# Lightning attention and a low-rank mixer: the state's product with 128 columns of weights, and mixing from two copies of V

## The chip, the cores and the metric
The kernel runs on one core of a Trainium2 chip. The metric is the time of one execution on the device, in microseconds (us).

## The reference
Four batches of 768 positions and 8 heads of 64 go through a decayed linear attention, in blocks of 64 positions. The result, read as x with 512 channels, is mixed along the sequence by a matrix of rank 32, and a two-layer network with a ReLU follows. Everything is fp32.

```python
for b in range(nb):                       # blocks of 64 positions, every head
    intra = einsum('bhic,bhjc->bhij', qb, kb) * Dmask       # decayed, causal
    intra = einsum('bhij,bhjd->bhid', intra, vb)
    inter = einsum('bhid,bhde->bhie', qb * lam_pow, kv_state)
    out[:, :, sl] = intra + inter
    kv_state = lam_block * kv_state + einsum('bhsd,bhse->bhde', kb_dec, vb)

x  = out.transpose(0, 2, 1, 3).reshape(4, 768, 512)
xt = x.transpose(0, 2, 1)
h  = xt @ U @ V                           # U: 768 x 32, V: 32 x 768
u  = x + h.transpose(0, 2, 1)
return u + maximum(u @ w_ch1, 0) @ w_ch2  # 512 -> 2048 -> 512
```

U, V and the two weights arrive as 8-byte floats, and the kernel makes fp32 values of them.

## The kernel before, in words
The kernel has three stretches. In the first (up to about 117 us) attention runs in `NS` = 24 steps s, each for 128 positions of one batch (c = s mod 6 counts the steps of a batch), and the mixing of the batch before runs between its pieces. In the second the first layer of the network runs, with matmuls of 128x128 weights against 512 columns, while the second layer's weights are prepared. In the third the second layer runs. Values that need more than the fast matmul type (`F32R`) holds are split in a high and a low part, and the products of the parts are summed.

In the first stretch the order on every engine is written out by hand: the loop that fills `pieces` lists the functions of a step, and each function issues its instructions at once. An engine works through its instructions in that order. For TensorE a middle step is: transposes of q and k for step s+1 (`prep`, L358), transposes of an earlier x (`turn`, L608), the mixing product of a step six or seven back (`mix`, L559), the masked scores times v (`intra`, L447), the new state (`state`, L425), the queries times the old state (`inter`, L458), and the scores of step s+1 (`scores`, L406). At the end of a batch `low` (L474) multiplies U by the batch's x.

The array of TensorE is used in parts. A form such as 64*128 in the profile says that weights of 64 rows and 128 columns are held. Heads lie in pairs: heads 2a and 2a+1 lie in the two halves of the 128 partitions (`half[x]`). `scores` uses 64*128: each half of the rows has one head's 64 channels, and the columns are 128 positions. `inter` uses 64*64: for each pair a and head x it issues one matmul for each half t of the 128 positions. It is left out in the first step of a batch (c = 0), where the state is zero. `px` takes both `intra` and `inter`, and ScalarE copies it to `x_nat` (L464), which frees it for the next step.

The mixing works in this way. `low_rows` splits the batch's low-rank part (32 x 512) into high and low parts and puts them in `p_hl`, a tile of 128 partitions x 512. For batches 0 to 2 the 512 channels are two halves of 256 that go to the two halves of the partitions. In each half the 32 rows of the high part stand twice, one below the other, in columns 0 to 255, and the 32 rows of the low part stand twice in columns 256 to 511. This is done by three small functions that `next_of_low` calls one after the other: `spread` (L527, four ScalarE casts), `low_part` (L531, two GpSimd subtractions) and `spread_low` (L538, two ScalarE casts). `v_hl` holds V in the four groups of 32 partitions: high, low, high, low. `mix` multiplies one 64-row half of V's 128 columns by each part of `p_hl`: four matmuls a step. `mixed` (L571, VectorE) adds the product to x. The last batch is mixed later, with one matmul of 128 rows a step (L566).

V is prepared by `v_steps` in the first steps: the loads, the conversion, then `five` (L699), the four ScalarE copies of its high part (L706), and the two calls of `low` (L710), of which one runs on VectorE and one on GpSimd. The table beside it puts both calls of `low` at the end of step 5. The first mixing product comes in step 7.

All loads and stores of this stretch go out through the queue of SyncE (SP), which takes its instructions in order: q, k and v of a later step (L279), the words of the weights (L140), and the stores of x (`u_d`, L577).

Of the kernel before, what the change touches and what calls it, by code (L numbers as in the profile page):

```python
# [8 lines left out]
FP32 = mybir.dt.float32  # L9
F32R = mybir.dt.float32r  # L10
# [4 lines left out]
P = 128  # L15
# [3 lines left out]
def kernel(  # L19
# [28 lines left out]
    nc = tc.nc  # L48

    B, H, S, D = q.shape  # L50
    HP = H // 2
    NT = S // P
    C = H * D
# [34 lines left out]
    def set_ends(t):  # L88
        nc.vector.memset(t[:, 0:1], 1151.0)
        nc.vector.memset(t[:, 1:2], 255.0 * (1 << 23))  # L90
        ends.append(t)
# [195 lines left out]

    assert G == 4
    vp = w1_pool.tile([P, 3, C], F32R, tag="w1", name="vp").rearrange("p n c -> p (n c)")
    v_hl, p_hl = vp[:, 0:S], vp[:, S : S + C]  # L290


    ident = keep.tile([P, P], FP32, name="ident")
    small = consts.tile([P, 16], FP32, name="small")
    zeros = small[:, 0:1]

    mask = consts.tile([P, 2, HP, P], FP32, name="mask")
# [154 lines left out]
    def inter(s):  # L452

        px = st[s]["px"][:, :, 0 : HP * D].rearrange("p x (a e) -> p x a e", a=HP)
        for a in range(HP if s % NT else 0):
            for x in range(2):
                for t in range(2):
                    nc.tensor.matmul(  # L458
                        out=px[half[t], x, a, :], lhsT=st[s]["qs"][half[x], a, half[t]],
                        rhs=kv[s][half[x], a, :], start=False, stop=(a == HP - 1),  # L460
                    )
        pool, tag = (att, "x10") if s % 10 == 5 else (x_pool, "x")
        xs[s] = pool.tile([P, C], FP32, tag=tag, name="x_nat")
        nc.scalar.copy(xs[s].rearrange("p (a x e) -> p x a e", a=HP, x=2), px)  # L464
        del st[s]
# [21 lines left out]
    def low_rows(b):  # L487

        pp, t = pps.pop(b), tmp("p_h")[0:R]
        own = [(slice(g * R, (g + 1) * R), slice(g * P, (g + 1) * P)) for g in range(G)]  # L490
        if b == B - 1:
            h, h2, l, l2 = (p_hl[g * R : (g + 1) * R] for g in range(G))
            for rows, cols in own:
                nc.vector.tensor_scalar(
                    t[:, cols].bitcast(U32), pp[rows].bitcast(U32), HI, None, ALU.bitwise_and
                )

            def low_part():
                for rows, cols in own:
                    nc.vector.tensor_tensor(  # L500
                        out=l[:, cols], in0=pp[rows], in1=t[:, cols], op=ALU.subtract
                    )

            def spread():
                nc.scalar.copy(h, t)
                nc.scalar.copy(h2, t)

            def spread_low():
                nc.scalar.copy(l2, l.bitcast(FP32))

            pps[b] = [spread, low_part, spread_low]
            return

        rows_f, pp = pp, others.pop(b)
        for g in range(2, G):
            nc.vector.tensor_copy(
                out=rows_f[:, g * P : (g + 1) * P], in_=pp[g * R : (g + 1) * R]
            )
        nc.vector.tensor_scalar(t.bitcast(U32), rows_f.bitcast(U32), HI, None, ALU.bitwise_and)
        wide = [slice(x * 2 * P, (x + 1) * 2 * P) for x in range(2)]  # L520

        def place(g, low):
            return p_hl[g * R : (g + 1) * R, wide[low]]

        def spread():
            for g in range(G):
                nc.scalar.copy(place(g, 0), t[:, wide[g // 2]])  # L527

        def low_part():
            for x in range(2):  # L530
                nc.gpsimd.tensor_tensor(  # L531
                    out=place(2 * x, 1), in0=rows_f[:, wide[x]], in1=t[:, wide[x]],
                    op=ALU.subtract,
                )

        def spread_low():
            for x in range(2):
                nc.scalar.copy(place(2 * x + 1, 1), place(2 * x, 1).bitcast(FP32))  # L538

        pps[b] = [spread, low_part, spread_low]  # L540

    def next_of_low(b):
        pps[b].pop(0)()
# [7 lines left out]

    def mix(s):
        b, c = divmod(s, NT)
        weights = v_hl[:, c * P : (c + 1) * P]
        if b < B - 1:
            pm = both_halves(s)[:, :, 2 * P :]
            for low in range(2):
                for x in range(2):
                    nc.tensor.matmul(  # L559
                        out=pm[:, x], lhsT=weights[half[x]],  # L560
                        rhs=p_hl[half[x], low * 2 * P : (low + 1) * 2 * P],
                        start=(low == 0), stop=(low == 1),
                    )
            return
        pu = bank([P, C], "pu", "b2")
        nc.tensor.matmul(out=pu, lhsT=weights, rhs=p_hl, start=True, stop=True)  # L566
        nc.vector.tensor_tensor(out=xs[s], in0=pu, in1=xs[s], op=ALU.add)

    def mixed(s):
# [68 lines left out]
    for s in range(NS):  # L638
        b, c = divmod(s, NT)
        done = s - NT - 1  # L640
        more = s + 1 < NS
        turns = done > 0 and (done - 1) // TG < FG
        mixes = 0 <= done < NS - NT - 1
        rows = c == 0 and b > 0
        step = [("prep", s + 1)] * more
        step += [("turn", done - 1)] * turns + [("mix", done)] * mixes
        step += [("mix", done + 1)] * (not more)
        step += [("next_of_low", b - 1)] * rows + [("next_of_low", b - 1)] * rows
        step += [("scale", s + 1)] * more
        step += [("fade", s)] * (c > 0)  # L650
        step += [("late", s - 1)] * (1 < s < NT - 1 or s > NT)
        step += [("turned", done - 2)] * (done > 1 and c == 1)
        step += [("split", done - 1)] * turns
        step += [("mixed", done)] * mixes + [("mixed", done + 1)] * (not more)
        step += [("next_of_low", b - 1)] * rows
        both = [("intra", s), ("state", s)]
        step += (both if s > NT else both[::-1]) + [("next_v", s), ("inter", s)]
        step += [("late", s)] * (s < 2 or s in (NT - 1, NT))
        step += [("turned", done - 1)] * (done > 0 and c > 0)
        step += [("scores", s + 1)] * more  # L660
        step += [("low", b)] * (more and c == NT - 1)
        step += [("aside", s)] * (0 < s < NT - 2 or s > NT)
        step += [("masked", s + 1)] * more
        step += [("low_rows", b)] * (more and c == NT - 1)
        step += [("aside", s)] * (s in (0, NT - 2, NT - 1, NT))
        step += [("store", done)] * (done >= 0 and done // TG < FG)
        pieces += step
# [14 lines left out]
    def v_steps():  # L682

        st = {}

        def dst():
            if "v" not in st:
                st["v"] = wconv.tile([P, C], FP32, tag="wf", name="vf")[0 : 2 * R, 0:SH]
            return st["v"]

        def parts(gs):
            for half in range(2):
                rows, cols = slice(half * R, (half + 1) * R), slice(half * SH, (half + 1) * SH)
                for g in gs:
                    yield v_hl[g * R : (g + 1) * R, cols], rows

        def five():
            st["t"] = t = wconv.tile([P, C], FP32, tag="wt", name="vt")[0 : 2 * R, 0:SH]
            nc.vector.tensor_scalar(  # L699
                t.bitcast(U32), st["v"].bitcast(U32), HI, None, ALU.bitwise_and  # L700
            )
            on_scalar(high)

        def high():
            for out, rows in parts((0, 2)):
                nc.scalar.copy(out, st["t"][rows])  # L706

        def low(g, engine):
            for out, rows in parts((g,)):
                engine.tensor_tensor(  # L710
                    out=out, in0=st["v"][rows], in1=st["t"][rows], op=ALU.subtract
                )

        halves = [moe_V[:, half * SH : (half + 1) * SH] for half in range(2)]
        return weight_steps(dst, halves, SH, 2 * R, in_parts=True) + [
            five, lambda: low(1, nc.vector), lambda: low(3, nc.gpsimd),
        ]
# [26 lines left out]

    ordered = ctx.enter_context(ExitStack())
    ordered.enter_context(tc.manual_schedule())
    lam_row = consts.tile([1, H + P], FP32, name="lam_row")
    blank = x_pool.tile([P, C], FP32, tag="x", name="blank")[:, 0:P]
    nc.vector.memset(blank, 0.0)
    nc.vector.memset(lam_row[:, H:], 1.0)  # L750
    set_ends(vp[:, S + C : S + C + 2].bitcast(FP32))
    nc.scalar.dma_start(out=lam_row[:, 0:H], in_=lam.unsqueeze(0))
    load_next("q", nc.sync)
    load_next("k", nc.scalar)
# [299 lines left out]
```

## Time and profile before

| | us |
|---|---|
| median of 3 runs | 667.36 (666.33 to 668.0) |
| the profiled execution | 669.62 |
| its span, first to last instruction | 667.8 |
| `intra` L447, 768 matmul records, mean | 0.225 |
| `inter` L458, 640 records, mean | 0.225 |
| `scores` L406, 384 records, mean | 0.291 |
| `mix` L559, 72 records, mean | 0.320 |
| ScalarE's casts to `p_hl`, L527 x12 and L538 x6, mean | 0.403 |

Matmuls are pipelined and their ends are modelled, so a mean is longer than the distance from one matmul to the next. How long a group holds TensorE is read from the starts of the groups in the order of time. A row of the order in time has the start, the length of the group, the engine, the line, the operation, the tiles written and read, the shapes and the number of records. PEld is the loading of weights, which goes on beside the matmuls.

### The profile page before, as it was taken

The numbers are of one execution on the slowest core, as the hardware profiler recorded it, in microseconds if no ns is written. First come the engines' busy times: TensorE is split into PE (matmuls) and PEld (weight loads), VectorE is DVE, ScalarE is ACT, GpSimd is POOL, SyncE is SP. The second block draws the span as 40 slices with busy tenths as digits, with TensorE's granted clock in tenths as the row PEclk, the third lists the DMA queues.
The fourth block names the chain that finished last, engine by engine and source line by source line (L and its number), as shares of the span: only waits on it lengthen the run. The fifth ranks groups of instructions, "written<-read, shape, count | busy, mean of one in ns | idle before, by whom it ended". The sixth has DMA issues, their size and how long they took to land.

```text
span 667.8 us, 13404 instructions
## 1 busy us (share of the span) xinstructions
PE 656.2 (98%) x5242; PEld 538.7 (81%) x5242; DVE 491.0 (74%) x862; ACT 280.4 (42%) x530; POOL 115.0 (17%) x98
## 2 busy tenths in 40 slices
PE   8899999999999999999999999999999999999997
PEld 7788988788888888888888887888888888888886
DVE  5578988878999777777797255786677776865864
ACT  4677885554555444444453121332322322322320
POOL 4465876330000000000000000030030300300300
PEclk9999999999999999999999999999999999999999
DMA  8999984355776655555578899764263453543531
GB/s 197 224 224 233 259 217 139 127 190 162 268 249 238 216 199 202 201 201 200 201 263 292 311 326 395 253 212 126 89 211 104 125 190 94 168 147 96 159 93 63
DMA packets 131776, 131.29 MB, mean 197 GB/s; under 512 B 81346, under 2 KB 89794, under 8 KB 131714
## 3 DMA queue, kind: packets, MB, share of 16 engines
q1 hardware_dynamic: 130512, 130.05, 62.2%
q8 instruction: 41, 0.67, 0.4%
q10 hardware_dynamic: 1202, 0.39, 0.2%
q14 instruction: 21, 0.17, 0.1%
HBM read 80.09 MB, written 50.33 MB: 195 GB/s over the span
## 4 chain that ended last, share of the span: by engine, by line
PE 95%; DMA 1%; DVE 1%; SPq 1%; issue 1%; ACT 0%; DVEq 0%; ACTq 0%
PE pz L817 27%; PE pz L950 13%; PE pz L952 13%; PE pd L827 13%; PE pd L954 13%; PE px L447 3%; PE pss L406 3%; PE px L458 2%; PE pqk L358 2%; DMA qraw<-in_q_dram 1%; PE pkv L425 1%; SPq L279 1%; PE pp L474 1%; PE pm L559 1%; PE put L590 1%
## 5 line engine op out<-in xcount | busy, mean ns | idle before, releaser
L817 PE MATMUL pz<-u_hl,w 128*128 128x512 f32 x768 | 190.0, 397 | 0.0
L817 PEld LDWEIGHTS pz<-u_hl,w 128*128 128x128 f32 x768 | 144.0, 188 | 35.2 <-ACT r L823 0.3
L952 PE MATMUL pz<-w_hl,m 128*128 128x512 f32 x384 | 151.1, 396 | 0.0
L950 PE MATMUL pz<-w_hl,m 128*128 128x512 f32 x384 | 150.9, 396 | 0.0
L954 PE MATMUL pd<-w_d,m 128*128 128x512 f32 x384 | 149.5, 396 | 0.0
L933 ACT ACTIVATE m<-mt 128x512 fp32r<-128x512 f32 x96 | 60.6, 632 | 196.6 <-PE pd L954 127.5
L979 POOL TENSOR_TENSOR o<-o,u 128x512 f32<-128x512 f32 x20 | 29.9, 1531 | 447.4 <-DMA rm<-r_d 291.4
L934 DVE SCALAR_TENSOR_TENSOR m<-rm,m 128x512 fp32r<-128x512 f32 x96 | 71.4, 745 | 47.3 <-ACT m L933 47.2
L832 DVE SCALAR_TENSOR_TENSOR r<-pd,r 128x512 f32<-128x512 f32 x96 | 61.8, 685 | 53.5 <-ACT r L823 43.5
L827 PE MATMUL pd<-u_d,w 128*128 128x512 f32 x384 | 98.6, 397 | 0.0
L823 ACT ACTIVATE r<-pz 128x512 f32<-128x512 f32 x96 | 52.1, 596 | 93.0 <-PE pz L817 92.3
L952 PEld LDWEIGHTS pz<-w_hl,m 128*128 128x128 f32 x384 | 72.3, 188 | 17.8 <-DVE m L934 0.2
L954 PEld LDWEIGHTS pd<-w_d,m 128*128 128x128 f32 x384 | 72.3, 188 | 17.7 <-DVE m L935 0.2
L950 PEld LDWEIGHTS pz<-w_hl,m 128*128 128x128 f32 x384 | 72.3, 188 | 17.6
L827 PEld LDWEIGHTS pd<-u_d,w 128*128 128x128 f32 x384 | 72.1, 188 | 17.3
L932 DVE TENSOR_SCALAR mt<-rm 128x512 uint32<-128x512 uint32 x96 | 46.1, 481 | 33.5 <-DMA rm<-r_d 33.2
L935 DVE SCALAR_TENSOR_TENSOR m<-m 128x512 fp32r<-128x512 f32 x96 | 69.1, 721 | 0.9
L415 DVE TENSOR_TENSOR sm<-pss,mask 128x512 f32<-128x512 f32 x48 | 30.9, 684 | 10.0 <-PE pss L406 9.7
L212 ACT CAST w<-wt 128x512 fp32r<-128x512 f32 x32 | 19.8, 620 | 30.6 <-DVE wt L209 23.4
L406 PE MATMUL pss<-qt,kt 64*128 64x128 f32 x384 | 29.1, 291 | 0.8 <-issue 0.7
L447 PE MATMUL px<-vraw,sm 128*64 128x64 f32 x768 | 27.8, 225 | 1.2 <-ACT x_nat L464 0.6
L447 PEld LDWEIGHTS px<-vraw,sm 128*64 128x64 f32 x768 | 24.9, 138 | 3.9 <-ACT x_nat L464 0.9
(96 smaller groups left out, 668.7 us busy)
## 6 DMA issues: line engine op xcount, KB each, us to landing
r_d<-r SPq DMA_DIRECT2D x96, 256.0 KB, 2.4
rm<-r_d SPq DMA_DIRECT2D x96, 256.0 KB, 2.7
words<-in_moe_w_ch_dram SPq DMA_DIRECT2D x30, 512.0 KB, 4.3
w_d<-w SPq DMA_DIRECT2D x16, 768.0 KB, 3.3
w_hl<-w_d SPq DMA_DIRECT2D x16, 512.0 KB, 6.4
vraw<-in_v_dram SPq DMA_DIRECT2D x24, 256.0 KB, 5.0
u_d<-x_nat SPq DMA_DIRECT2D x24, 256.0 KB, 4.1
u<-u_d SPq DMA_DIRECT2D x24, 256.0 KB, 4.1
```

Source lines behind the costliest of these rows:

```text
L406: nc.tensor.matmul(out=pss[:, x, a, :], lhsT=kt[half[x], a, :], rhs=qt[half[x], a, :], start=True, stop=True,)
L447: nc.tensor.matmul(out=px[half[t], x, a, :], lhsT=sm[:, x, a, half[t]], rhs=vr[:, 2 * a + x, :], start=(a == 0), stop=(alone and a == HP - 1),
L817: nc.tensor.matmul(out=acc[g][0], lhsT=w[:, n, ct, :], rhs=uhl[g][:, n, ct, :], start=(ct == 0 and n == 0), stop=(ct == CT - 1 and n == 1),)
L823: nc.scalar.mul(rs[g], acc[g][0], 4096.0 + 1.0)
L827: nc.tensor.matmul(out=acc[g][1], lhsT=w[:, 2, ct, :], rhs=ud[g][:, ct, :], start=(ct == 0), stop=(ct == CT - 1),)
L832: nc.vector.scalar_tensor_tensor(rs[g], acc[g][1], 4096.0, rs[g], ALU.mult, ALU.add)
L933: nc.scalar.activation(out=m[:, 0], in_=t, func=AF.Relu)
L934: nc.vector.scalar_tensor_tensor(m[:, 1], r, 0.0, hi, ALU.max, ALU.subtract)
L935: nc.vector.scalar_tensor_tensor(m[:, 2], hi, E, low, ALU.mult, ALU.subtract)
L950: nc.tensor.matmul(out=pz, lhsT=m[:, 0, cols], rhs=hl[:, 0], start=first, stop=False)
L952: nc.tensor.matmul(out=pz, lhsT=m[:, 1, cols], rhs=hl[:, 1], start=False, stop=end)
L954: nc.tensor.matmul(out=pd, lhsT=m[:, 2, cols], rhs=dd, start=first, stop=end)
```

## The change
Three things are changed in the first stretch.

`inter` issues one matmul for each pair a and head x with all 128 positions as columns of weights. It has 8 matmuls a step where it had 16.

`mix` keeps its four matmuls but multiplies another pairing. `v_hl` becomes 128 x 2 x 768: in copy 0 the groups are V's high, low, high, low as before, in copy 1 they are low, high, low, high. `p_hl` becomes 128 x 256, with high and low one below the other in each half of the partitions. One matmul with copy 0 gives high x high and low x low, and one with copy 1 gives low x high and high x low. Copy 1 is made by four DMAs from copy 0 within SBUF (`swap`), issued on SP at the head of step 6. `spread` has two casts in place of four, and `spread_low` is gone.

The places of some small things move: `p_hl` gets a tile of its own, the row for `lam` goes to an unused part of the tile `blank`, and the two constants of `set_ends` go to the tile `small`. The last batch puts its low-rank part where copy 1 of V was.

```diff
-    v_hl, p_hl = vp[:, 0:S], vp[:, S : S + C]
+    v_hl = vp.rearrange("p (n c) -> p n c", n=2)
+    p_hl = consts.tile([P, 2 * P], F32R, name="p_hl")
...
-    small = consts.tile([P, 16], FP32, name="small")
+    small = consts.tile([P, 18], FP32, name="small")
...
             for x in range(2):
-                for t in range(2):
-                    nc.tensor.matmul(
-                        out=px[half[t], x, a, :], lhsT=st[s]["qs"][half[x], a, half[t]],
-                        rhs=kv[s][half[x], a, :], start=False, stop=(a == HP - 1),
-                    )
+                nc.tensor.matmul(
+                    out=px[:, x, a, :], lhsT=st[s]["qs"][half[x], a, :],
+                    rhs=kv[s][half[x], a, :], start=False, stop=(a == HP - 1),
+                )
...
-            h, h2, l, l2 = (p_hl[g * R : (g + 1) * R] for g in range(G))
+            h, h2, l, l2 = (v_hl[g * R : (g + 1) * R, 1, 0:C] for g in range(G))
...
-        def place(g, low):
-            return p_hl[g * R : (g + 1) * R, wide[low]]
+        def place(g):
+            return p_hl[g * R : (g + 1) * R]
 
         def spread():
-            for g in range(G):
-                nc.scalar.copy(place(g, 0), t[:, wide[g // 2]])
+            for x in range(2):
+                nc.scalar.copy(place(2 * x), t[:, wide[x]])
 
         def low_part():
             for x in range(2):
                 nc.gpsimd.tensor_tensor(
-                    out=place(2 * x, 1), in0=rows_f[:, wide[x]], in1=t[:, wide[x]],
+                    out=place(2 * x + 1), in0=rows_f[:, wide[x]], in1=t[:, wide[x]],
                     op=ALU.subtract,
                 )
 
-        def spread_low():
-            for x in range(2):
-                nc.scalar.copy(place(2 * x + 1, 1), place(2 * x, 1).bitcast(FP32))
-
-        pps[b] = [spread, low_part, spread_low]
+        pps[b] = [spread, low_part]
...
-        weights = v_hl[:, c * P : (c + 1) * P]
+        weights = v_hl[:, :, c * P : (c + 1) * P]
         if b < B - 1:
             pm = both_halves(s)[:, :, 2 * P :]
-            for low in range(2):
+            for n in range(2):
                 for x in range(2):
                     nc.tensor.matmul(
-                        out=pm[:, x], lhsT=weights[half[x]],
-                        rhs=p_hl[half[x], low * 2 * P : (low + 1) * 2 * P],
-                        start=(low == 0), stop=(low == 1),
+                        out=pm[:, x], lhsT=weights[half[x], n], rhs=p_hl[half[x]],
+                        start=(n == 0), stop=(n == 1),
                     )
             return
         pu = bank([P, C], "pu", "b2")
-        nc.tensor.matmul(out=pu, lhsT=weights, rhs=p_hl, start=True, stop=True)
+        nc.tensor.matmul(out=pu, lhsT=weights[:, 0], rhs=v_hl[:, 1, 0:C], start=True, stop=True)
...
-        step = [("prep", s + 1)] * more
+        step = [("swap", s)] * (s == NT) + [("prep", s + 1)] * more
...
-        step += [("next_of_low", b - 1)] * rows
...
+        def swap():
+            whole = v_hl.bitcast(FP32)
+            for g in range(G):
+                nc.sync.dma_start(
+                    out=whole[g * R : (g + 1) * R, 1],
+                    in_=whole[(g ^ 1) * R : ((g ^ 1) + 1) * R, 0],
+                )
...
-    lam_row = consts.tile([1, H + P], FP32, name="lam_row")
-    blank = x_pool.tile([P, C], FP32, tag="x", name="blank")[:, 0:P]
+    blank = x_pool.tile([P, C], FP32, tag="x", name="blank")
+    lam_row, blank = blank[0:1, P : P + H + P], blank[:, 0:P]
...
-    set_ends(vp[:, S + C : S + C + 2].bitcast(FP32))
+    set_ends(small[:, 16:18])
```

More of the change, by code (lines that the diff above doesn't have):

```diff
@@ L694, in parts @@
                 for g in gs:
-                    yield v_hl[g * R : (g + 1) * R, cols], rows
+                    yield v_hl[g * R : (g + 1) * R, 0, cols], rows
         def five():
@@ L712, in low @@
                 )
+        def swap():
[5 more added lines that the diff above has]
+                )
+        run["swap"] = lambda s: swap()
         halves = [moe_V[:, half * SH : (half + 1) * SH] for half in range(2)]
```

## The prediction

> **What bounds the kernel now.** I read the page first: the busy table and the forty slices, then the chain that ended last. They say that TensorE sets the end from the first slice to the last, at full clock.
>
> ```profile
> PE 656.2 (98%) x5242; PEld 538.7 (81%) x5242; DVE 491.0 (74%) x862; ACT 280.4 (42%) x530; POOL 115.0 (17%) x98
> PEclk9999999999999999999999999999999999999999
> PE 95%; DMA 1%; DVE 1%; SPq 1%; issue 1%; ACT 0%; DVEq 0%; ACTq 0%
> ```
>
> The change lies in the attention part, the first 117 us of 667.8. So next came the chain of waits there, then the order of instructions in one undisturbed step (24 steps of 128 positions; this is step 16).
>
> ```profile
> 82.66 1.15 PE L447 MATMUL px<-vraw,sm 128*64 128x64 f32 x32
> 83.64 0.64 PE L425 MATMUL pkv<-vraw,ks 128*64 128x64 f32 x16
> 84.21 0.69 PE L458 MATMUL px<-kv,qs 64*64 64x64 f32 x32
> 84.83 1.16 PE L406 MATMUL pss<-qt,kt 64*128 64x128 f32 x16
> 85.83 0.41 PE L358 MATMUL pqk<-ident,qraw 64*128 64x64 f32 x8
> ```
>
> One row follows another; a step is about 4.3 us of TensorE. The state's part (L458) holds it from 84.21 to 84.83, 0.62 us; the scores behind it from 84.83 to 85.83, 1.00 us. Each fp32 matmul is two instructions here (640 records for 320 matmuls). The last view is the weight loads at the head of three rows, each asked for in a window cut short after the row begins:
>
> ```profile
> 84.20 0.20 PEld L458 LDWEIGHTS px<-kv,qs 64*64 64x64 f32 x6
> 84.83 0.30 PEld L406 LDWEIGHTS pss<-qt,kt 64*128 64x128 f32 x4
> 89.76 0.15 PEld L474 LDWEIGHTS pp<-x_nat,u_w 128*32 128x32 f32 x7
> 86.01 0.33 PEld L358 LDWEIGHTS pqk<-ident,kraw 64*128 64x128 f32 x8
> ```
>
> Columns: start, length, group, count. A record of the four forms lasts 0.135, 0.188, 0.11 and 0.145 us, so the last record in each line starts at length minus that. Loads to different parts of the array start together (four parts in the first line, two in the second, four in the third), and the next group begins 0.20-0.135 = 0.06, 0.30-0.188 = 0.11 and 0.15-0.11 = 0.04 us after the first. **So a group of loads takes about 0.06 us with 64 columns, 0.11 with 128, 0.03 to 0.04 with 32: it goes by columns.** The fourth line, a transpose, is the exception: four pairs of 128 columns, 0.33-0.145 = 0.19 us for three intervals, 0.06 each.
>
> **What the Trainium skill says.** "TensorE: Matmul & The Clock Gate", section "LDWEIGHTS (loading the stationary operand)": a load costs its columns divided by 1.2 in ns, whatever the rows, so 53 and 107 ns for 64 and 128. The trace agrees (0.06 and 0.11). "TensorEngine Tiling (Array Packing)", "Key Properties": changing the tiling mode drains TensorE. The trace agrees: L447 to L425, same tiling, is 0.98 us above; the same 32 instructions followed by another tiling take 1.08 (86.96 to 88.04 in the next step), so a switch costs about 0.10. "DMA: Bandwidth & Descriptors", "Anatomy of one DMA": a DMA's semaphore wait is served on the issuing sequencer before dispatch. The trace shows waits on SP's queue of up to 5.1 us, with later issues behind them.
>
> **The state's part.** Before: 32 instructions in eight groups of four (two row halves, two column halves). 0.06 for the first load, 8 x 0.06 = 0.48 for the groups, 0.09 for the switch into the scores: 0.62. The scores: 0.11 for the first load and 8 pairs x 0.112 = 0.89, together 1.00. Both: 1.62 us.
> After: 16 instructions in eight pairs, the weights 64 rows x 128 columns, exactly the form of L406, the moving side 64 columns. The moving side of a pair needs half of L406's, about 0.055. But its weights need 0.11[...], so a pair takes 0.11, whatever the matmul takes. No switch lies between it and the scores, so the two rows run as 16 pairs: 0.11 + 16 x 0.112 = 1.90 us. **A loss of 0.28 a step.** It halves the instructions and saves one switch of 0.09, but doubles the time of the loads that the four-part tiling took in parallel. Bounds: if the loads ran at the transposes' 0.06, the two would take 0.06 + 8 x 0.06 + 8 x 0.112 = 1.44, a gain of 0.18. I take the loss, since L406 has the identical load and shows 0.11 for it.
> There are 20 such steps (c > 0). In step 1, TensorE waits for q's DMA right after the scores (the chain has the DMA up to 16.59), which hides it. 19 x 0.28 = **+5.3 us**, on the path.
>
> **The swapped copy of V.** New: four DMAs within SBUF, 32 partitions x 3,072 bytes, at the head of step 6, on SP. They need all of V's split, and the first mix, in step 7, needs them.
>
> ```profile
> 37.87 1.55 DVE L710 TENSOR_TENSOR vp<-vf,vt 32x384 fp32r<-32x384 f32 x2
> 38.01 1.45 SPq L140 DMA_DIRECT2D words<-in_moe_w_ch_dram  x1
> 39.54 1.32 SPq L279 DMA_DIRECT2D qraw<-in_q_dram  x1
> 39.89 0.83 ACT L538 CAST vp<-vp 32x256 fp32r<-32x256 f32 x2
> 40.08 1.07 PE L559 MATMUL pm<-vp 64*128 64x256 f32 x4
> 41.38 1.15 PE L447 MATMUL px<-vraw,sm 128*64 128x64 f32 x32 [0.23 <-ACT x_nat L464]
> ```
>
> V's last low part ends on DVE at 39.42. SP then issues four DMAs of about 0.4 us (the shortest issues in this view), to about 41.1. No small copy inside SBUF is in this trace; bounds for its landing are 0.5 us (nothing ahead, bytes only: 98 KB at 250 GB/s) and 4.4 (the words' median here). I take 1.9, a little under the 2.4 of the 256 KB stores of r, so 43.0. The mix's second half would have been ready at 40.2; it now starts near 43.0, and L447 of step 7 follows near 43.3 instead of 41.38: **+1.9 us**, once, with ends -0.4 and +5. TensorE is in order, so scores, transposes and all else queue behind that mix; on SP, the q and k loads of step 7 and later queue behind the swap's wait, but they are issued three steps ahead, some 13 us, against a landing of 4 to 5, so I cost them at nothing; without that cover, up to 1.6 us of issue once.
>
> **The low-rank part kept once.** Each of batches 0 to 2 loses four ACT casts of 0.40 us (two of L527, two of L538), 1.6 us of ACT, and one wait of ACT on POOL. In step 6 this frees the 0.4 us for which L559 waits on L538 and L447 on x_nat; the swap above covers it, and it is counted there. At 65 and 92 us the chain goes through p_f, p_h, ut, u_hl and x_nat on DVE, which stay; ACT is not in it after p_f, so nothing is gained. The mix itself keeps its four instructions of 64x256 and its loads: 0. The other moved pieces (lam_row, the two end constants, p_hl in another pool) lie in the first 16 us, bounded by q's loads ("DMA qraw<-in_q_dram", 8.97 us of the chain): 0; without that cover, some 0.2 us for a wait at the warm-up matmuls.
>
> **Instruction supply.** The chain of the first 300 us has 1.9% in "issue", about 5.5 us, in pieces of 0.7 to 1.6 us on TensorE. L458 gives up 320 matmul and 320 load records, of some 5,700 that TensorE has before 117 us (the counts of the attention's groups, twice 2,850). In proportion, 5.5 x 640/5,700 = **-0.6 us**; ends 0 and -2.5.
> **Slack.** Where TensorE waits for ACT (before the L447 at 78.27: 0.75 us after L559's start, elsewhere 0.42) a slower TensorE lets ACT catch up: -0.3.
>
> Sum: 5.3 + 1.9 - 0.6 - 0.3 = **+6.3 us**. From 117 us on nothing changes, and TensorE is full there, so the shift goes through to the end. The profiled execution took 669.62 us (span 667.8 and 1.8 around it); it would become 675.9. It stands 2.3 above the median of the runs, 667.36; I put the difference on the median: **673.7 us**.
>
> **Rivals.**
> 1. *The swap is hidden* (lands by 41): 5.3 - 0.4 - 0.6 - 0.3 = +4.0, 671.4. For it: only 0.4 MB, no HBM. Against: DVE's L710 ends 0.7 us before the mix is due.
> 2. *The swap's wait is long*, landing at 46 and beyond. Then TensorE may idle over 3.4 us, and the first page named above ("Part 1: The HAM clock gate") says an idle window of that length halves the clock until it is busy again for as long. No run here shows it: the longest gap, 1.86 us at 25, left the clock at 1.00. 5.3 + 5 + 1.7 (half of 3.4) - 0.9 = +11.1, 678.5. For it: the DMA rows at 38 to 41 us are full.
> 3. *The loads aren't the limit* (the other side). If 64x128 loads beside a short moving side run as in the transposes, each step gains 0.18 instead of losing: 19 x -0.18 + 1.9 - 0.6 - 0.3 = -2.4, 665.0. It decides from the pair time p at which the two layouts are level, 9p + 0.90 = 1.62, so 0.08 us; at 0.074 the whole change is level. Against: the identical load in L406.
>
> **Chances.** Forecast 0.60, rival 1 0.13, rival 2 0.12, rival 3 0.15. A measurement of this kernel tells a change from none at about 0.3%, 2 us. Rival 3 splits: 0.09 faster by more, 0.06 within. Half of the spread of rival 1 towards zero gives 0.03 more within. Slower 0.82, same 0.09, faster 0.09. Range 668.5 to 678.0: its low end takes in rival 1 with fewer supply stalls (-2.5), its top the long landing without the clock; rival 3 and the end of rival 2 stay out. The likeliest case alone has 671.5 to 676.5.
>
> **What would show it.** L458's group in 64*128 form with 320 records, a row of about 0.99 us from its start to the scores' start, and 0.9 (not 1.00) for the scores. L559 at 40 us waiting for a DMA written on vp, about 2 to 3 us. L538 gone, L527 halved, no change at 65 and 92 us. An L458 row of 0.5 us would prove rival 3 and break the forecast; a first mix without a DMA wait proves rival 1.

## The result, and the profile after

| | before | changed |
|---|---|---|
| median, us | 667.17 (666.33 to 668.0, 4 runs) | 676.25 (673.61 to 678.58, 4 runs) |
| profiled execution, us | 669.62 | 678.58 |
| span of it, us | 667.8 | 676.8 |

The ratio is 1.0137 (95% interval 1.0101 to 1.0173), 9.1 us at the medians. It was forecast at 673.7, between 668.5 and 678.0. The time is inside; the make-up of it isn't quite what was forecast, as the traces show. The four runs of the changed kernel took 678.6 and 677.2 us at a mean granted clock of 0.992, and 675.3 and 673.6 us at 0.997 and 0.996; the profiled execution is the first of these, so its loss by the clock is at the high end.

The page of the changed kernel first: busy time by engine, the clock granted to TensorE in forty slices of 16.9 us, and the chain that ended last.

```profile
PE 665.1 (98%) x4922; PEld 549.3 (81%) x4922; DVE 491.6 (73%) x862; ACT 275.5 (41%) x518; POOL 114.4 (17%) x98
PEclk9988999999999999999999999999999999999999
PE 95%; DMA 2%; DVE 1%; ACT 1%; issue 0%; SPq 0%; ACTq 0%; DVEq 0%
```

TensorE has 320 matmul records fewer (160 fp32 matmuls of two records each) and is busy 8.9 us longer. Two slices, from 34 to 68 us, have a lower clock, and "issue", 1% before, is gone from the chain, while DMA has a point more.

An undisturbed middle step of the changed kernel (step 14; steps 13 and 15 have the same length) in the order of time, TensorE alone, and below it the weight loads in a window cut short after L458 begins:

```profile
82.13 1.15 PE L448 MATMUL px<-vraw,sm 128*64 128x64 f32 x32
83.11 0.64 PE L426 MATMUL pkv<-vraw,ks 128*64 128x64 f32 x16
83.68 1.11 PE L458 MATMUL px<-kv,qs 64*128 64x64 f32 x16
84.62 1.11 PE L407 MATMUL pss<-qt,kt 64*128 64x128 f32 x16
85.57 0.41 PE L359 MATMUL pqk<-ident,qraw 64*128 64x64 f32 x8
```

```profile
83.68 0.30 PEld L458 LDWEIGHTS px<-kv,qs 64*128 64x128 f32 x4
```

The state's part holds TensorE from 83.68 to 84.62 and the scores to 85.57: 0.94 and 0.95, together 1.89 us where 1.62 stood before. The load's line is the scores' line of before: four records of 0.19 us in 0.30, so the second pair begins 0.11 us after the first.

The place of the swap, steps 6 and 7, in the order of time (L711 is the swap, L704 V's low parts, L555 the first mix):

```profile
38.27 1.54 DVE L704 TENSOR_TENSOR vp<-vf,vt 32x384 fp32r<-32x384 f32 x2
39.84 3.12 SPq L711 DMA_DIRECT2D vp<-vp  x4
40.48 0.41 PE L555 MATMUL pm<-p_hl,vp 64*128 64x256 f32 x2
43.05 0.54 SPq L279 DMA_DIRECT2D qraw<-in_q_dram  x1
43.49 0.38 PE L555 MATMUL pm<-p_hl,vp 64*128 64x256 f32 x1 [2.60 <-DMA vp<-vp]
44.71 0.55 PE L555 MATMUL pm<-p_hl,vp 64*128 64x256 f32 x1 [0.84 <-DMA vp<-vp]
45.19 1.97 PE L448 MATMUL px<-vraw,sm 128*64 128x64 f32 x32
```

The first two matmuls of the mix take copy 0 and run at 40.48 (each is one record here). The other two wait for copy 1, 2.60 and 0.84 us. L448 of step 7 begins at 45.19 (41.38 before) and is 1.97 long where 1.15 is usual. The stretches around it show why; after the bounds come the busy times of the engines with their counts, and PEclk, the share of the clock granted:

```profile
35.00:41.00 6.00, 5.62 (x146) 4.97 (x143) 4.93 (x10) 4.78 (x12) 3.32 (x4) 1.00 1.01 238
41.00:44.80 3.80, 0.47 (x2) 0.30 (x2) 0.59 (x1) 1.79 (x6) 3.00 (x3) 0.93 0.58 133
44.80:55.00 10.20, 10.20 (x145) 9.64 (x147) 3.79 (x7) 2.61 (x7) 2.34 (x2) 0.52 0.92 225
55.00:65.00 10.00, 10.00 (x242) 9.53 (x240) 9.21 (x16) 7.52 (x18) 5.97 (x5) 1.00 0.83 214
```

The clock record of this trace has half clock from 44.3 to 54.5 us, which is why the rows cut at 44.8 and 55 have 0.93 and 0.52. From 44.8 on TensorE is never idle, and yet the row up to 55 us has 145 matmul records, where the ten microseconds after it have 242.

The 8.85 us by which the first matmul of the first layer starts later (117.36 and 126.21) can be laid out by the starts of the masked scores' product (L447 before, L448 after):

```
stretch                        before   after   later by
start to step 6                 37.54   37.93     0.39   five state rows (1.35), 0.96 given back
step 6 to step 7                 3.84    7.26     3.42   the wait for the swap
step 7 to step 9                 8.65   13.32     4.67   two state rows (0.54), half clock (4.1)
step 9 to step 23               65.54   65.50    -0.04   twelve state rows (3.24), 3.28 given back
step 23 to the first layer       1.79    2.20     0.41   one state row (0.27)
```

The waits and the state rows (0.27 each) are read from the trace; the half clock and what is given back are what is left over. So the state's part costs 5.4 us gross and the swap 7.5, and some 4 us come back in this pair of executions. The 0.96 of the first stretch should not be leaned on: that stretch is 36.4 to 38.4 us long in the profiled executions of kernels with 128 columns. The 3.28 lie in single steps that had waits before and have none after (steps 9 and 21 above all). The view of waits, TensorE only, up to the first layer: its longest rows before were

```profile
PE pqk L358 <- issue: 1.6, 1, 1.6
PE px L458 <- issue: 0.9, 1, 0.9
PE pkv L425 <- issue: 0.8, 1, 0.8
PE pqk L358 <- DMA qraw<-in_q_dram: 0.7, 2, 0.5
PE pss L406 <- issue: 0.7, 1, 0.7
```

(waiter, what it waited for, us, times, longest), 4.0 us of "issue" in all from 9 us on; after the change "issue" is 0.3. "Issue" says only that the profile shows nothing that TensorE waited for. New in the changed kernel, beside the swap, are 2.2 us of waits for v's DMA in steps 3 and 4, ahead of the swap; there are none before, 0.5 us with the state's part alone, and 2.7 and 2.2 us in the two kernels without the swap below. What brings them was not tested.

### The profile page after: what moved, and what is told of

It reads as the page before. It is cut to its first block, busy times and chain, and to the rows that moved or that the text cites. A ratio compares the mean times of both kernels' runs of the same rounds, so it can differ in the third digit from the quotient of the medians.

```text
span 676.8 us, 12769 instructions
## 1 busy us (share of the span) xinstructions
PE 665.1 (98%) x4922; PEld 549.3 (81%) x4922; DVE 491.6 (73%) x862; ACT 275.5 (41%) x518; POOL 114.4 (17%) x98
## 4 chain that ended last, share of the span: by engine, by line
PE 95%; DMA 2%; DVE 1%; ACT 1%; issue 0%; SPq 0%; ACTq 0%; DVEq 0%
PE pz L820 27%; PE pz L953 13%; PE pz L955 13%; PE pd L830 13%; PE pd L957 13%; PE px L448 4%; PE px L458 3%; PE pss L407 3%; PE pqk L359 2%; PE pkv L426 1%; DMA vraw<-in_v_dram 1%; PE pm L555 1%; PE pp L474 1%; PE pm L603 1%; DMA kraw<-in_k_dram 1%; PE put L585 1%
## 5 line engine op out<-in xcount | busy, mean ns | idle before, releaser
L982 POOL TENSOR_TENSOR o<-o,u 128x512 f32<-128x512 f32 x20 | 29.8, 1527 | 447.5 <-DVE o L978 447.5
L416 DVE TENSOR_TENSOR sm<-pss,mask 128x512 f32<-128x512 f32 x48 | 30.9, 685 | 14.7 <-PE pss L407 14.6
L448 PE MATMUL px<-vraw,sm 128*64 128x64 f32 x768 | 29.2, 231 | 1.0 <-issue 0.3
L448 PEld LDWEIGHTS px<-vraw,sm 128*64 128x64 f32 x768 | 26.3, 144 | 3.9 <-issue 1.1
```

Of the source, the lines that this page charges most:

```text
L448: nc.tensor.matmul(out=px[half[t], x, a, :], lhsT=sm[:, x, a, half[t]], rhs=vr[:, 2 * a + x, :], start=(a == 0), stop=(alone and a == HP - 1),
```

## The experiments

Twelve kernels, in four groups. Each group was timed against the kernel before on the same chip, whose median there was 668.9 to 670.1, so ratios are compared, not times. The first four take the two large parts of the change apart.

**The state's part alone**, in the kernel before.

```diff
-                for t in range(2):
-                    nc.tensor.matmul(
-                        out=px[half[t], x, a, :], lhsT=st[s]["qs"][half[x], a, half[t]],
...
+                nc.tensor.matmul(
+                    out=px[:, x, a, :], lhsT=st[s]["qs"][half[x], a, :],
```

> Only the state's part of the change, in the kernel before: one matmul with 128 columns of weights in place of two with 64. Theory A (a pair is held by its weight loads, 0.11 us whatever the moving side takes): the state's row is about 0.94 us, the scores' 0.95, together 0.27 more than the 1.62 of before in each of 20 steps, and the time is up by 4 to 5.5 us, to about 671.5 to 672.5, no DMA wait at the first mix, clock 1.00. Rival (the change's cost is nearly all the swap and the clock drop behind it; the state's row is neutral where TensorE has slack): within 1.5 us of before.

Ratio 1.0012 (0.9989 to 1.0035). An undisturbed step takes 4.57 us where it took 4.30, as theory A has it, and yet the first layer starts at 118.06, only 0.7 later than before. TensorE's waits up to there sum to 1.8 us, 5.8 before. The longest rows now are

```profile
PE px L447 <- issue: 0.6, 2, 0.3
PE px L447 <- DMA vraw<-in_v_dram: 0.5, 1, 0.5
PE px L447 <- DVE p_f L515: 0.3, 1, 0.3
```

Theory A is right about the row and wrong about the time, where the rival's number holds: of 5.4 us some 4.5 are given back (3.1 to 6.1 by the interval of the ratio).

**The change with the state's part undone** (the same edit the other way).

> The change with the state's part put back to 64 columns. Theory A: 4.5 to 5.5 us faster than the changed kernel, so about 671 (669 to 673 by how long the clock stays down), still slower than before by 2 to 5 us; the first mix still waits 3 to 4 us on the swap, and the clock still falls. Rival (state's part neutral): about 675 to 676, as the changed kernel.

Ratio 1.0087 (1.0061 to 1.0114), 0.5% under the changed kernel's, some 3.4 us if both ratios are taken at their middle; the intervals overlap. That lies between theory A (4.5 to 5.5 us) and the rival (about none), and with both intervals, some 0 to 6 us, it settles neither. The mix waits 4.9 us on the swap, and the clock is half for 6.8 us.

**The wait filled with work**: 18 matmuls of the identity ahead of the first mix.

```diff
+            if s == 0:
+                idle = two_banks("idle", "pm")[:, 0]
+                for i in range(18):
+                    nc.tensor.matmul(
+                        out=idle[:, 0:P], lhsT=ident, rhs=ident, start=True, stop=True
+                    )
```

> The changed kernel with 18 more matmuls of the identity with itself ahead of the first mix, about 4 us of useless work on TensorE where it waits for the swap. Theory A (the wait lets the clock fall, and the half clock costs 2 to 4 us on top of the wait): the clock stays at 1.00, the slots after 45 us run at full rate, and the time falls to about 672 to 673. Rival (the idle time itself is the whole cost, and the clock's fall is made up in later slack): the same 676, or slower by what the extra matmuls overrun.

Ratio 1.0079 (1.0060 to 1.0099), 0.58% or 3.9 us under the changed kernel's. The order of time and the stretch after it:

```profile
39.06 4.29 PE L555 MATMUL idle<-ident 128*128 128x128 f32 x36
39.15 3.06 SPq L717 DMA_DIRECT2D vp<-vp  x4
43.49 0.82 PE L561 MATMUL pm<-p_hl,vp 64*128 64x256 f32 x4
```

```profile
45.00:55.00 10.00, 10.00 (x248) 9.53 (x244) 7.29 (x15) 5.72 (x16) 5.68 (x5) 1.00 0.93 221
```

The same wait (7.86 us from step 6 to step 7, 7.26 in the changed kernel), spent on useless matmuls, leaves the clock at 1.00, with 248 matmul records from 45 to 55 us. Work was added and time was saved: the half clock is a cost of its own, of about 4 us (1 to 7 by the two intervals).

**The first mix without copy 1.**

```diff
-                        out=pm[:, x], lhsT=weights[half[x], n], rhs=p_hl[half[x]],
+                        out=pm[:, x], lhsT=weights[half[x], n * (s > 0)], rhs=p_hl[half[x]],
```

> The changed kernel, but the first mix (step 7) takes copy 0 of V in both of its products, so that one tile of positions gets a wrong cross term; its work is the same and it does not wait for the swap, which has a whole step more. Theory A: wait (3 to 3.5 us) and clock drop (2 to 4) go, so 676.3 falls to about 669.5 to 671, which is the kernel before plus the state's part (5) less some us of fewer instruction stalls. Rival (swap's DMAs and the waits on SP cost elsewhere, the wait is moved to the next mix): 673 or more.

Ratio 1.0099 (1.0066 to 1.0132): the rival's. Step 7 now takes 3.16 us, but step 9 takes 7.56. In the order of time (L160 and L149 convert the weights' words, L416 makes the masked scores that L448 needs):

```profile
44.63 0.94 SPq L140 DMA_DIRECT2D words<-in_moe_w_ch_dram  x1
50.04 0.79 DVE L160 TENSOR_SCALAR sc<-words 128x512 uint32<-128x512 uint32 x1 [2.04 <-DMA words<-in_moe_w_ch_dram]
50.76 1.49 DVE L149 TENSOR_SCALAR m<-words 128x512 uint32<-128x512 uint32 x1
52.16 1.27 DVE L416 TENSOR_TENSOR sm<-pss,mask 128x512 f32<-128x512 f32 x2
52.94 0.55 PE L448 MATMUL px<-vraw,sm 128*64 128x64 f32 x5 [2.92 <-ACT sc L167]
```

The swap holds SP for 2.8 us, so the words go out at 44.63 (42.55 before). VectorE waits 2.04 us for them with the masked scores behind it, and TensorE waits 2.92 for those. The row names ScalarE, which came last by the profile; the masked scores are what L448 reads. The clock falls there too, for 3.4 us. Taking one wait away showed the next.

**Half of the moving side** in the changed kernel's state matmuls.

```diff
-                    out=px[:, x, a, :], lhsT=st[s]["qs"][half[x], a, :],
-                    rhs=kv[s][half[x], a, :], start=False, stop=(a == HP - 1),
+                    out=px[:, x, a, 0 : D // 2], lhsT=st[s]["qs"][half[x], a, :],
+                    rhs=kv[s][half[x], a, 0 : D // 2], start=False, stop=(a == HP - 1),
```

> The changed kernel, but the state's matmuls take only 32 of the 64 columns of the moving side, so half of the state's contribution is left out. Theory A (a pair is held by its weight loads): the row of L458 stays at 0.94 us from its start to the scores' start. Rival (the moving side or the number of results holds a pair): the row falls towards 0.6 to 0.7 us.

One run, read for its rows alone. TensorE in the order of time, at full clock:

```profile
93.10 1.08 PE L458 MATMUL px<-kv,qs 64*128 64x32 f32 x16
94.01 1.14 PE L407 MATMUL pss<-qt,kt 64*128 64x128 f32 x16
94.99 0.41 PE L359 MATMUL pqk<-ident,qraw 64*128 64x64 f32 x8
```

From L458's start to the transposes' start 1.89 us, as with the whole moving side (the first row is 0.03 shorter, the second as much longer). The loads hold the row; the moving side doesn't.

**Without the swap**, with 128 and with 64 columns in the state's part.

```diff
-        step = [("swap", s)] * (s == NT) + [("prep", s + 1)] * more
+        step = [("prep", s + 1)] * more
...
-                        out=pm[:, x], lhsT=weights[half[x], n], rhs=p_hl[half[x]],
+                        out=pm[:, x], lhsT=weights[half[x], 0], rhs=p_hl[half[x]],
```

> The changed kernel without the four DMAs of the swap; every mix of the first three batches takes copy 0 of V twice, so the cross terms of high and low are left out or wrong. Theory B (what the change costs is the swap: its wait, the clock behind it, and its 3 us on SP that make the weights' words and v late; the state's part is paid back by fewer stalls): the time is that of the state's part alone, 669.5 to 671 where before has 668.9, no clock drop. Theory A with a cost of 5 us for the state's part: 673 to 674.

> As the run without the swap, and the state's part put back to 64 columns: only the low-rank part kept once is left of the change (cross terms again left out or wrong). Theory B: within 1 us of before, as ScalarE is not what ends the steps; the instruction stalls of before come back. Rival (the casts taken from ScalarE are worth something): 1 to 2 us faster than before.

Ratios 0.9999 (0.9983 to 1.0016) and 0.9986 (0.9969 to 1.0004). Without its swap the change costs nothing that can be measured. The swap is thus worth 1.4% with 128 columns and 1.0% with 64 (1.0137 against 0.9999, 1.0087 against 0.9986). The state's part is worth about 0.13% here, as it was alone (0.12%): about 1 us of 5.4, with an interval of some 1.6 us to either side. The low-rank part kept once is at most 2 us of gain and perhaps nothing, by the second interval.

One thing here went against what I had expected: with 64 columns the stalls of before did not come back. "Issue" is 0.6 us in that profiled execution, and the first layer begins at 114.65, 4.2 us ahead of the kernel with 128 columns (118.84), while the medians are 1.2 us apart. Over all these kernels, the filler apart, the profiled executions with 64 columns have 4.0, 1.8, 0.6, 3.0 and 0.2 us of "issue" up to the first layer, those with 128 columns 0.0 to 0.8. So with 64 columns the stalls differ from one execution to the next, and how much the wider weights give back is read from the ratios, not from one pair of traces.

**A filler in the kernel before**, to tell whether a slower step or the smaller number of instructions takes the stalls away.

```diff
+        if s % NT:
+            idle = two_banks("idle", "pss")[:, 0, 0:160]
+            nc.tensor.matmul(
+                out=idle, lhsT=ident[half[0]],
+                rhs=powq.rearrange("p a i -> p (a i)")[half[0], 0:160], start=True, stop=True,
+            )
```

> The kernel before with one useless fp32 matmul of 64x128 weights and 160 moving columns between the state's part and the scores, about 0.27 us of TensorE in each of 20 steps: the slower step of the change without its smaller number of instructions. Theory C (the first stretch has about 4 us of stalls of TensorE in 'issue' that go when it asks for instructions more slowly, whatever their number): the time is up by 0.5 to 2 us, as with the state's part alone. Theory D (only the 640 records less take the stalls away): up by about 5 us, the stalls still there.

Ratio 1.0114 (1.0092 to 1.0135), 7.6 us. But the filler holds TensorE 0.59 us a step, not 0.27 (it starts at 91.55, the scores behind it at 92.14), so 11.8 us went in and some 4 came back. TensorE's waits fall to 2.7 us, 2.3 of them "issue", with as many instructions as before and a few more. That fits a slower step alone taking part of the stalls away, but as executions with 64 columns differ by as much, and as the filler's size was off, the run settles neither theory.

**The swap moved out of the way**: low parts of V a step earlier, the DMAs on GpSimd's queue, with 128 and 64 columns.

```diff
-        (v_steps(), (0, 0, 3, 3, 4, 4, 4, 5, 5)),
+        (v_steps(), (0, 0, 3, 3, 4, 4, 4, 4, 4)),
...
-                nc.sync.dma_start(
+                nc.gpsimd.dma_start(
```

> The changed kernel with both low parts of V made at the end of step 4 and the four DMAs of the swap issued on GpSimd's queue in place of SP's. GpSimd has an idle stretch of about 2.5 us before its work for the low-rank part, and SP's loads are not held up. Theory B (the swap costs 7 to 9 us by its place: the wait at the first mix, the clock behind it, SP's queue): the swap lands before the first mix at 40 us or within 1 us of it, the clock stays at 1.00, and the time is 669 to 671, a ratio of 1.000 to 1.003 to before, as without the swap. Rival (four DMAs within SBUF cost the loads beside them as much wherever they are issued): ratio 1.006 or more.

> As the run with the hidden swap, with the state's part put back to 64 columns. Theory B: about 1 us faster than with 128 columns, so a ratio of 0.997 to 1.000 to before. If the state's part costs its whole 5 us once the swap's wait is gone: a ratio of 0.992 to 0.995. Rival (128 columns are no worse when the stalls are counted): the two runs agree within 0.1%.

Ratios 1.0102 (1.0072 to 1.0131) and 1.0063 (1.0044 to 1.0082): it isn't hidden. Four rows of the order of time, with 128 columns:

```profile
36.72 2.34 POOL L711 DMA_DIRECT2D vp<-vp  x4
40.70 0.78 PE L555 MATMUL pm<-p_hl,vp 64*128 64x256 f32 x2 [0.42 <-POOL p_hl L531]
44.08 0.55 PE L555 MATMUL pm<-p_hl,vp 64*128 64x256 f32 x1 [2.60 <-DMA vp<-vp]
44.55 1.98 PE L448 MATMUL px<-vraw,sm 128*64 128x64 f32 x32
```

The DMAs are issued three microseconds earlier, but land 4.3 us after their issue in the median (2.7 on SP), and the mix's last matmul starts at 44.08 where it started at 44.71. TensorE waits, and the clock falls as before. Why they land later on this queue isn't shown.

**Copy 1 written by the engines** from V's split, no DMA, with 128 and 64 columns.

```diff
+        def other():
+            for half in range(2):
+                rows, cols = slice(half * R, (half + 1) * R), slice(half * SH, (half + 1) * SH)
+                for grp, engine in ((0, nc.vector), (2, nc.gpsimd)):
+                    engine.tensor_tensor(
+                        out=v_hl[grp * R : (grp + 1) * R, 1, cols],
+                        in0=st["v"][rows], in1=st["t"][rows], op=ALU.subtract,
+                    )
+                for grp in (1, 3):
+                    nc.vector.tensor_copy(
+                        out=v_hl[grp * R : (grp + 1) * R, 1, cols], in_=st["t"][rows]
+                    )
```

> The changed kernel, with copy 1 of V written by the engines from V's split (VectorE 1.5 us of subtractions and about 1.6 us of casts, GpSimd 2 us, at the end of step 5) in place of the four DMAs; copy 0's low parts are made a step earlier. All of the change's arithmetic is there, no DMA. Theory B (the swap's latency and what follows it are nearly all of the change's cost): no DMA wait at the first mix, clock at 1.00, ratio 1.000 to 1.003 to before. Rival (the mixing from two copies itself costs): ratio above 1.006.

> As the run with the copies made by the engines, with the state's part put back to 64 columns. Theory B: 0.1 to 0.2% less than with 128 columns, so a ratio of 0.997 to 1.001 to before. If the state's part costs its whole 5 us here: 0.992 to 0.995.

Ratios 1.0121 (1.0096 to 1.0147) and 1.0064 (1.0042 to 1.0087). The numbers are the rival's, but not for its reason. VectorE in the order of time:

```profile
39.17 1.34 DVE L712 TENSOR_TENSOR vp<-vf,vt 32x384 fp32r<-32x384 f32 x1
40.52 1.60 DVE L717 CAST vp<-vt 32x384 fp32r<-32x384 f32 x2
42.13 1.52 DVE L712 TENSOR_TENSOR vp<-vf,vt 32x384 fp32r<-32x384 f32 x1
43.66 2.46 DVE L717 CAST vp<-vt 32x384 fp32r<-32x384 f32 x2
46.73 0.89 PE L555 MATMUL pm<-p_hl,vp 64*128 64x256 f32 x4 [5.70 <-DVE kv L432]
```

Six instructions, for which I had put 3.1 us, take 6.9, and the first mix waits 5.70 us behind them (the row names L432, the VectorE instruction that follows them at once). The clock falls here also, to half for 10.2 us. The wait has another source and the same price. None of these kernels beats the one before by more than its interval.

## Why the prediction was right, and where it was not

**What bounds it, and the order of reading: right.** TensorE is the bound, and each large item of the change was found in its row.

**The state's part: right in its row.** A pair of loads takes 0.11 us, the two rows 1.89 us (forecast 1.90), 0.27 a step (0.28). The run with half of the moving side shows that it is the load, as the section "LDWEIGHTS (loading the stationary operand)" of the Trainium skill's "TensorE: Matmul & The Clock Gate" has it by columns. Rival 3 is out. Why the transposes load pairs of 128 columns in 0.06 us, as the prediction noted, stays open.

**Instruction supply and slack: mis-sized.** They were put at -0.6 and -0.3 us; about 4 came back in the changed kernel and some 4.5 in the state's part alone. The proportion with the records was the wrong measure: what went were whole stalls of 0.7 to 1.6 us. That they go because TensorE asks later is a reading, not shown, since the filler left it open and one execution with 64 columns had hardly any. Nor is it shown that these were waits for instructions, as the term's name has it.

**The swap: right in kind, short in size.** I had it landing at 43.0; it landed at about 44.7. SP took 3.12 us for its four DMAs and not 1.6, and the landing took 2.7 in the median and not 1.9. The term is 3.4 us against 1.9. On GpSimd's queue and by the engines the wait stayed; only without the swap was it gone, and nearly all of the 9 us with it.

**The clock: the step that failed.** "The swap's wait is long" was rival 2, at 0.12, and asked for a landing at 46 or later. A wait of 2.60 and 0.84 us with one matmul between them was enough, and the cost is 4.1 us in the profiled execution, not the 1.7 put there. The filled wait shows the mechanism. The longest idle gap before, 1.64 us (the prediction's 1.86 counts from start to start), had left the clock at 1.00. "Part 1: The HAM clock gate" of the same page speaks of an idle window of about 3.4 us. Here less was enough: TensorE was busy for 0.4 us of the 3.4 before the fall, and in the run without the first wait one gap of 2.92 us brought the clock down. The prediction took the half clock to last 3.4 us; it lasted 10.2.

**SP's queue: wrong.** I costed the loads behind the swap at nothing, as they are issued three steps ahead. The words of the weights aren't issued so early: the run without the first wait lost 2.9 us at step 9 through VectorE. In the changed kernel the wait at step 7 covers it.

**The low-rank part: right**, no change at 65 and 92 us (73 and 102 after), and a gain that cannot be told from none.

So +6.3 against +9.1 is right in sign and within the range, but in part by luck, since two errors offset each other: swap and clock came out 5.6 us dearer, the stalls gave about 3 more back. The top of the range had left the clock out.

What stays open: with a wait at the first mix, 128 columns cost 0.4 to 0.6% against 64 (1.0137 and 1.0087, 1.0102 and 1.0063, 1.0121 and 1.0064), without it 0.13%, all with wide intervals. A longer half clock with the longer row is one reading. The profiled executions fit it: from step 7 to step 9 they take 13.3, 13.3 and 12.9 us with 128 columns and 10.1, 9.8 and 10.4 with 64, where two state rows are 0.54. But executions of one kernel differ among themselves, with mean clocks from 0.991 to 0.997 in both forms, so it isn't shown.

## What to carry to other kernels

Before merging column parts of the array into wider ones, compare the load of a group with its moving side: here, with 128 weight columns and only 64 columns moving, the load set the pace, and half the instructions brought nothing in the row. Read the load's rate from a matmul of the same kind, as this kernel's transposes have another. A one-time transfer is priced by what waits for it, by the queue that it holds, and by the clock: here a wait of 3.4 us on TensorE cost 4.1 us more by the clock. Stalls in the stretch that a change slows are part of its price; they may vanish and take most of a true loss with them. As they can differ from one execution to the next, read that from many runs and not from one trace.

## What the runs showed of the hardware

A gap of 2.60 and 0.84 us on TensorE was followed by 10.2 us at half clock, though TensorE was busy from the gap's end on. In the eight profiled executions in which the clock fell, it was half for 10.2 us four times (all with 128 columns), 6.8 twice and 3.4 twice, always once, twice or three times the same 3.41. Counted in the clock record's own steps of 3.41 us, TensorE had been busy for 0.9 us or less of the step before each fall (0.4 in the changed kernel, from 40.9 to 44.3). The least busy step that left the clock at 1.00 had 2.1 us (without the swap, from 26.4 to 29.8). Nothing here at full clock lies between.

Four DMAs of 96 KB within SBUF took 0.78 us each to issue on SP between loads (3.12 for four) and 2.7 us to land in the median; on GpSimd's queue, beside SP's loads, 4.3 us.

A cast of 32x384 on VectorE took 0.80 to 1.23 us in the stretch where it was tried, where I had put 0.4.

Loads of weights of 64x128 for fp32 matmuls went at 0.11 us a pair, with 64 and with 32 columns moving. Four loads of 64x64 to the four parts of the array took 0.06 us together.
